# Moving the third block product ahead of the first set of output products in each pair of a gated unit

## The chip, the cores and the metric

The kernel runs on one core of a Trainium2 chip. The metric is the time of one execution in device microseconds (us). Before the change the median of 3 runs is 873.7 us (872.63 to 873.97).

## The reference, cut to what matters

The kernel computes three layers: windowed attention, a mixture of experts with one expert for each token, and a gated unit. The change lies in the gated unit:

```python
def _moe2_ref(x, w_gate, w_val, w_out, rms_g):      # 2304 tokens, 512 wide, 1536 hidden
    rms = np.sqrt(np.mean(x * x, axis=-1, keepdims=True) + 1e-06)
    xn = x / rms * rms_g
    g = xn @ w_gate
    silu = g * (1.0 / (1.0 + np.exp(-g)))
    val = xn @ w_val
    return (silu * val @ w_out).astype(np.float32)
```

## The kernel before, in words

The gated unit takes the tokens in 6 chunks of 384 (`c` = 0 to 5) and the 1536 hidden columns in 12 blocks of 128 (`f`). Every float32 operand is held as a high and a low float16 part, and a product is the sum of three products of parts. Chunks 0 and 1 are computed plainly (`plain`). Chunks 2 to 5 go through `quad(c, p)`, which takes hidden blocks 2p and 2p+1 together: 6 pairs in a chunk, 24 pairs in all. A pair is a two by two block product, and seven block products, named 1 to 7, give it instead of eight. One block product (`product`, L1014 to L1025) is 12 matmuls of 128x192 into one PSUM bank: gate and value, two halves of the contraction, three products of parts.

VectorE (DVE) puts the seven results together with additions (`add`, L1092). Product 1 is first copied to `u0` by ScalarE (L1110). `one` becomes hidden block 2p, `other` block 2p+1, each with a left and a right half of the tokens. The last addition of a pair is that of product 4 into the left half of `other` (L1126). Then `gated` (L1100) makes the activation: Silu on ScalarE (L1101), a multiply on VectorE (L1102), the high part on ScalarE (L1096) and the low part on VectorE (L1097).

The output products of a finished hidden block are one set of 9 matmuls of 128x512: three row blocks by three products of parts, added up in three banks over all 12 hidden blocks of a chunk (`down`, L1130). `downs` (L1214) takes the oldest block that waits in `pending`. A pair calls it twice, so that in its first set stands block 2(p-1) and in its second block 2(p-1)+1 of the pair before. The set of a chunk's last block falls into the second place of the next chunk's first pair; there the three results are copied to rows (`o`, L1142 and L1144) and scattered to the output. The first set of that chunk's second pair then begins the next sums in the same three banks.

Work for the next chunk is put between (`side_work`, L1267): loads in pair 0, maxima (L970, L487) in pair 1, the scale (L491, L495) in pair 2, transposes (`gtx`, L983) in pair 3, sums of the rows (L995 to L998) and splits into parts (L926 on ScalarE, L927 on VectorE) in pairs 4 and 5. The longest split, of 1536 columns, stands in pair 5 just ahead of `add(other[:, :, :HT], product(c, p, "4"), u)`.

The order on every engine is the order in which the program is written. The seven products use two PSUM buffer tags of two buffers each, and a tag's buffers are handed out in turn:

```python
PAIRS = {"1": (0, 0), "2": (1, 1), "3": (6, 2), "4": (2, 6), "5": (3, 3), "6": (4, 4), "7": (5, 5)}
acc = bank("a" if x in "1634" else "d", "g" + x)        # BANKS: "a": 2, "d": 2
```

Within a pair tag a is asked for by products 1, 6, 3 and 4 in this order, so that 1 and 3 lie in one of its banks, 6 and 4 in the other. A product's first matmul waits until the bank's last reader is done: product 6 of a pair waits for the addition of product 4 of the pair before, product 3 for the copy to `u0`, product 4 for the addition of product 6.

Of the kernel before, what the change touches and what calls it, by code (L numbers as in the profile page):

```python
# [74 lines left out]
def attn_moe_glu(tc, I, out, dbg=None):  # L75
    nc = tc.nc
    with contextlib.ExitStack() as top:
# [58 lines left out]
        def block_tile(name):  # L136
            return tail.tile([P, D], F32, name=name, tag="block", bufs=2)
# [34 lines left out]
        def bank(name, use=None):  # L172
            return ps.tile([P, 512], F32, name=use or name, tag=name, bufs=BANKS[name])
# [840 lines left out]
        def product(c, p, x):  # L1014

            i, j = PAIRS[x]
            acc = bank("a" if x in "1634" else "d", "g" + x)
            for gv in range(2):
                for m in range(2):
                    for n, (a, b) in enumerate(((0, 0), (0, 1), (1, 0))):  # L1020
                        nc.tensor.matmul(  # L1021
                            acc[:, gv * HT : gv * HT + HT], GV[p][:, a, gv, i, m * P : m * P + P], XC[c][:, b, j, m],
                            start=m == 0 and n == 0, stop=m == 1 and n == 2,
                        )
            return acc[:, :CHT].rearrange("p (g t) -> p g t", g=2)  # L1025
# [66 lines left out]
        add = lambda out, x, y: nc.vector.tensor_tensor(out, x, y, ALU.add)  # L1092
# [7 lines left out]
        def gated(c, f, g, v, si):  # L1100
            nc.scalar.activation(si, g, AF.Silu, scale=undo[:, c % 2, 0:1])  # L1101
            nc.vector.scalar_tensor_tensor(si, v, undo[:, c % 2, 1:2], si, ALU.mult, ALU.mult)  # L1102
            act_split(c, f, si)

        def quad(c, p, downs, work, last):

            p1, p2 = (product(c, p, x) for x in "12")
            u0, u = (block_tile(x)[:, :CHT].rearrange("p (g t) -> p g t", g=2) for x in ("u0", "u"))
            one, other = (g2.tile([P, 2, CHT], F32, name=x) for x in ("one", "other"))
            nc.scalar.activation(u0, p1, AF.Copy)  # L1110
            add(one[:, :, :HT], p2, u0)
            next(work, None)
            downs()
            add(u, product(c, p, "6"), u0)
            p5 = product(c, p, "5")
            add(one[:, :, HT:], p5, u)
            next(work, None)
            p3 = product(c, p, "3")
            add(one[:, :, HT:], p3, one[:, :, HT:])
            add(u, product(c, p, "7"), u)  # L1120
            add(other[:, :, HT:], p5, u)
            gated(c, 2 * p, one[:, 0], one[:, 1], one[:, 0])
            next(work, None)
            if not last:
                downs()
            add(other[:, :, :HT], product(c, p, "4"), u)  # L1126
            next(work, None)
            gated(c, 2 * p + 1, other[:, 0], other[:, 1], other[:, 0])

        def down(c, f, j):  # L1130
            ahi, alo = acts[c, f]
            acc = ACC[c][j]
            cols = slice(j * P, j * P + P)
            for n, (a, part) in enumerate(((ahi, 0), (ahi, 1), (alo, 2))):
                nc.tensor.matmul(  # L1135
                    acc, a[:, cols], GO[f][part],
                    start=f == 0 and n == 0, stop=f == NFF - 1 and n == 2,
                )
            if f == NFF - 1:
                o = row_tile("o")[:, :D]  # L1140
                if j % 2:
                    nc.vector.tensor_scalar(o, acc, undo[:, c % 2, 2:3], None, ALU.mult)  # L1142
                else:
                    nc.scalar.activation(o, acc, AF.Copy, scale=undo[:, c % 2, 2:3])  # L1144
                d = scatter(out, IX[c][j], o).ins
                for x in written:
                    tc.declare_no_dep(d, x, reason="the rows differ")
                written.append(d)
# [65 lines left out]
        def downs(last=False):  # L1214

            if pending:
                c, f = pending.pop(0)
                if f == 0:
                    ACC[c] = [bank(x, "acc") for x in "bbc"]
                for j in blocks:  # L1220
                    down(c, f, j)
# [82 lines left out]
        for c in range(PLAIN, NCH):  # L1304
            for p in range(NP):
                work = side_work(c, p)
                last = (c, p) == (NCH - 1, NP - 1)
                quad(c, p, downs, work, last)
                for _ in work:
                    pass  # L1310
                pending += [(c, 2 * p), (c, 2 * p + 1)]
        table = over["table"]

        c = NCH - 1
# [100 lines left out]
```

## Time and profile before

| | |
|---|---|
| median of 3 runs | 873.7 us |
| profiled execution | 880.13 us, of which the span of the trace is 878.3 us |
| TensorE matmuls (PE) | busy 839.8 us, 96% of the span |
| TensorE weight loads (PEld) | 652.4 us, 74% |
| VectorE (DVE) | 594.4 us, 68% |
| ScalarE (ACT) | 408.4 us, 47% |
| GpSimd (POOL) | 175.2 us, 20% |
| block products, L1021 | 2016 matmuls, first at 592.7 us, last at 858.4 us |

All times of rows are us from the start of the span. A timeline row gives start, duration, engine, line, operation, output and inputs, a count where equal neighbours are put together, and in brackets the idle time ahead of it with what ended it. Matmuls overlap: a row of 12 times n block product matmuls is shown some 0.16 us longer than the distance to the next row. "PEclk" is the granted TensorE clock: 1.00 is 2.4 GHz, 0.50 is 1.2 GHz.

### The profile page before, as it was taken

How to read it: one execution, taken by the hardware profiler on the slowest of the kernel's cores; microseconds unless marked ns; L12 is line 12 of the kernel's file. 1: busy time of each engine (PE TensorE's matmuls, PEld its weight loads, DVE VectorE, ACT ScalarE, POOL GpSimd, SP SyncE). 2: the span in 40 equal slices, each digit the busy share in tenths (PEclk: the TensorE clock that was granted, in tenths of full speed). 3: DMA queues.
4: the chain of work that ended last, by engine and by line, in shares of the span. 5: the costliest groups of instructions: out<-in, count | busy, mean ns of one | idle time of the engine just before them, and what ended most of it. 6: DMA issues, size and time to landing. Idle time of an engine off the chain costs nothing.

```text
span 878.3 us, 17260 instructions
## 1 busy us (share of the span) xinstructions
PE 839.8 (96%) x5927; PEld 652.4 (74%) x5927; DVE 594.4 (68%) x1647; ACT 408.4 (47%) x957; POOL 175.2 (20%) x206
## 2 busy tenths in 40 slices
PE   8999979999899999999899999899999999999994
PEld 6888878987788888888755555458787887778882
DVE  7657848798988887534456747666676666667752
ACT  6867759856445455322445534343233233233221
POOL 3644118532343333200000001001001001001001
PEclk9969989999999999999999999999999999999998
DMA  9994579426877776250055006201001000000001
GB/s 215 260 282 93 140 230 295 125 62 217 243 249 230 230 217 202 73 168 24 13 192 183 34 31 257 97 13 61 13 1 61 13 2 37 2 1 37 1 2 38
DMA packets 100470, 101.96 MB, mean 116 GB/s; under 512 B 63136, under 2 KB 75424, under 8 KB 100384
## 3 DMA queue, kind: packets, MB, share of 16 engines
q1 hardware_dynamic: 92848, 86.34, 33.3%
q0 software_dynamic: 4400, 14.20, 4.2%
q8 instruction: 52, 0.85, 0.4%
q10 hardware_dynamic: 3136, 0.30, 0.3%
q14 instruction: 34, 0.28, 0.1%
HBM read 67.18 MB, written 33.89 MB: 115 GB/s over the span
## 4 chain that ended last, share of the span: by engine, by line
issue 43%; PE 41%; DVE 8%; DMA 3%; ACT 2%; POOL 1%; POOLq 0%; SPq 0%; ACTq 0%; DVEq 0%
PE h L657 10%; PE y L682 10%; PE s L233 3%; PE g L1021 3%; PE xp L337 3%; PE xp L339 2%; DVE pb L261 2%; PE acc L1135 2%; PE mth L633 1%; PE few L369 1%; PE pt L302 1%; POOL out L710 1%; DMA yd<-yn,ix 1%; PE mtx L633 1%; DMA xd<-xs,pli 1%
## 5 line engine op out<-in xcount | busy, mean ns | idle before, releaser
L1021 PEld LDWEIGHTS <-gv 128*128 128x128 f16 x2016 | 167.7, 98 | 11.2
L1021 PE MATMUL g<-xc,gv 128*128 128x192 f16 x2016 | 175.0, 246 | 0.0
L710 POOL DMA_INDIRECT out<-o,ix x18 | 18.1, 1004 | 397.8 <-ACT o L1144 395.1
L682 PE MATMUL y<-W,hhi 128*128 x304 | 96.1, 397 | 0.0
L1037 PE MATMUL gv<-xn,gv 128*128 128x384 f16 x528 | 90.6, 326 | 1.3 <-DVE one L1102 0.7
L657 PE MATMUL h<-W,xhi 128*128 x272 | 90.0, 412 | 0.1
L1135 PE MATMUL acc<-go,alo 128*128 128x512 f16 x216 | 81.9, 379 | 0.0
L1037 PEld LDWEIGHTS <-gv 128*128 128x128 f16 x528 | 51.5, 98 | 37.9 <-issue 2.4
L272 ACT ACTIVATE pb<-pb,mn 128x256 f32<-128x256 f32 (+4 forms) x160 | 74.4, 468 | 10.7 <-DVE mn L261 10.0
L1135 PEld LDWEIGHTS <-ahi 128*128 128x128 f16 x432 | 41.4, 98 | 41.9 <-issue 3.4
L261 DVE CUSTOM_DVE_ANT_0 pb<-s,bias 128x256 f32<-128x256 f32 (+4 forms) x160 | 53.6, 380 | 23.4 <-PE s L233 22.5
L682 PEld LDWEIGHTS y<-W,hhi 128*128 128x128 f32 x304 | 57.4, 189 | 14.0
L1135 PE MATMUL acc<-gv,ahi 128*128 128x512 f16 x216 | 64.3, 379 | 3.5 <-ACT o L1144 1.8
L1135 PE MATMUL acc<-go,ahi 128*128 128x512 f16 x216 | 64.3, 379 | 0.7 <-ACT ahi L1096 0.7
L746 POOL TENSOR_TENSOR cw<-cw,cv 128x512 int32<-128x512 int32 x36 | 47.1, 1310 | 69.7 <-DVE cw L745 27.1
L682 PE MATMUL y<-W,hlo 128*128 x152 | 60.1, 396 | 0.0
L657 PEld LDWEIGHTS h<-W,xhi 128*128 128x128 f32 x272 | 49.1, 191 | 9.8 <-issue 0.4
L657 PE MATMUL h<-W,xlo 128*128 x136 | 54.6, 402 | 0.0
L1101 ACT ACTIVATE one<-one,undo 128x384 f32<-128x384 f32 x24 | 14.8, 615 | 83.7 <-DVE one L1092 83.7
L692 ACT ACTIVATE yn<-y,xg 128x512 f32<-128x512 f32 x19 | 13.1, 690 | 84.1 <-PE y L682 84.1
L1096 ACT ACTIVATE ahi<-one 128x384 f16<-128x384 f32 x36 | 18.8, 523 | 55.7 <-DVE one L1102 55.7
L233 PE MATMUL s<-kT,qT 64*128 64x256 f32 (+1 forms) x288 | 42.1, 404 | 0.3 <-ACT kT L203 0.2
(273 smaller groups left out, 1649.1 us busy)
## 6 DMA issues: line engine op xcount, KB each, us to landing
raw<-gd SPq DMA_DIRECT2D x20, 768.0 KB, 5.4
gd<-cw SPq DMA_DIRECT2D x36, 256.0 KB, 2.9
W<-in_moe_w SPq DMA_DIRECT2D x16, 512.0 KB, 5.9
cv<-in_moe_w_gate SPq DMA_DIRECT2D x12, 512.0 KB, 4.6
cv<-in_moe_w_val SPq DMA_DIRECT2D x12, 512.0 KB, 4.8
cv<-in_moe_w_out SPq DMA_DIRECT2D x12, 512.0 KB, 4.5
xd<-zrow SPq DMA_DIRECT2D x20, 257.0 KB, 5.5
xg<-xd SPq DMA_DIRECT2D x19, 257.0 KB, 3.2
```

The lines of the kernel that those rows point to most:

```text
L233: nc.tensor.matmul(sps[j][:, u, :W], qT[rows, i], win(i, j), start=True, stop=True)
L261: nc.vector.tensor_tensor_reduce(pb[rw, u, x0:x1], sp[rw, u, x0:x1], bias[rw, h, b0 + x0 : b0 + x1], 1.0, 3.0e38, ALU.add, ALU.min, M[t][0 ...
L272: nc.scalar.activation(pb[rw, u, x0:x1], pb[rw, u, x0:x1], AF.Exp, bias=mn[rw, h : h + 1], scale=-1.0, accum_out=sm[rw, h : h + 1],)
L337: nc.tensor.matmul(X[t][:, h], cur, T["v", t][:, h], start=True, stop=not full)
L657: nc.tensor.matmul(hp[f], x[:, k], WT[1][k][:, ds(w, 1), part, f * 512 : f * 512 + 512], start=k == 0 and n == 0, stop=k == KD - 1 and n == 2,
L682: nc.tensor.matmul(y, x[:, k], WT[2][k // 2][:, ds(w, 1), part, k % 2 * D : k % 2 * D + D], start=k == 0 and x is hi and part == 0, stop=k ...
L710: return nc.gpsimd.indirect_dma_start(dst[:, :], bass.IndirectOffsetOnAxis(ap=ix[:, 0:1], axis=0), src, None, bounds_check=NTOK - 1, oob_i ...
L746: nc.gpsimd.tensor_tensor(ci, ci, low.bitcast(I32), ALU.add)
L1021: nc.tensor.matmul(acc[:, gv * HT : gv * HT + HT], GV[p][:, a, gv, i, m * P : m * P + P], XC[c][:, b, j, m], start=m == 0 and n == 0, stop ...
L1037: nc.tensor.matmul(acc[:, :CHT], w[:, m * P : m * P + P], XC[c][b][:, k], start=k == 0 and n == 0, stop=k == KD - 1 and n == 2,)
L1096: nc.scalar.activation(ahi, si, AF.Copy, scale=2.0**-LOW)
L1135: nc.tensor.matmul(acc, a[:, cols], GO[f][part], start=f == 0 and n == 0, stop=f == NFF - 1 and n == 2,)
```

## The change

In `quad`, the block product 6 and its addition are issued ahead of the first set of output products instead of behind it.

```diff
             nc.scalar.activation(u0, p1, AF.Copy)
             add(one[:, :, :HT], p2, u0)
             next(work, None)
+            add(u, product(c, p, "6"), u0)
             downs()
-            add(u, product(c, p, "6"), u0)
             p5 = product(c, p, "5")
             add(one[:, :, HT:], p5, u)
             next(work, None)
```

On TensorE, at the first pair of chunk 3. `g4`, `g1`, `g2`, `g6`, `g5` are the block products, `acc` the output products; of each group of matmuls the first one is shown, and a line of dots stands for the rest. Before:

```order
L1021 MATMUL g4_7697<-xc_6786,gv5_6018 128x192
...
L1021 MATMUL g1_7717<-xc_7548,gv0_5415 128x192
...
L1021 MATMUL g2_7730<-xc_7548,gv0_5415 128x192
...
L1135 MATMUL acc_7022<-gv5_6018,ahi0_7682 128x512
...
L1021 MATMUL g6_7764<-xc_7548,gv0_5415 128x192
...
L1021 MATMUL g5_7778<-xc_7548,gv0_5415 128x192
```

With the change:

```order
L1021 MATMUL g4_7697<-xc_6786,gv5_6018 128x192
...
L1021 MATMUL g1_7717<-xc_7548,gv0_5415 128x192
...
L1021 MATMUL g2_7730<-xc_7548,gv0_5415 128x192
...
L1021 MATMUL g6_7755<-xc_7548,gv0_5415 128x192
...
L1135 MATMUL acc_7036<-gv5_6018,ahi0_7682 128x512
...
L1021 MATMUL g5_7778<-xc_7548,gv0_5415 128x192
```

The 12 matmuls of `g6` moved ahead of the 9 of the set; between `g4` and `g6`, which share a bank, stand now two block products and no set. The same holds in all 24 pairs.

On VectorE, at the end of chunk 2 and the beginning of chunk 3, the order is the same before and with the change (the rows are those of before):

```order
L1097 SCALAR_TENSOR_TENSOR alo0_7683<-ahi0_7682,one_7608 128x384
L927 SCALAR_TENSOR_TENSOR xc_7548<-tt_7471,up2_2901,xc_7548 128x1536
L1092 TENSOR_TENSOR other_7609<-g4_7697,u_7607 128x2x192
L1102 SCALAR_TENSOR_TENSOR other_7609<-other_7609,undo_2904 128x384
L1097 SCALAR_TENSOR_TENSOR alo1_7714<-ahi1_7713,other_7609 128x384
L1092 TENSOR_TENSOR one_7745<-g2_7730,u0_7743 128x2x192
```

Nothing moved here: the longest split stands ahead of the addition of `g4`, which `g6` waits for. The only row that moves on VectorE is in the first of the 24 pairs, where the addition of product 6 now stands ahead of the copy of an output row:

```order
 L1092 TENSOR_TENSOR one<-g_6857,u_6870 128x2x192
+L1092 TENSOR_TENSOR u<-g_6882,u_6870 128x384
 L1142 TENSOR_SCALAR o<-acc,undo 128x512
-L1092 TENSOR_TENSOR u<-g_6906,u_6870 128x384
 L1092 TENSOR_TENSOR one<-g_6920,u 128x2x192
```

ScalarE, GpSimd and the DMA queues keep their order.

## Rows read from the trace of the kernel before

**Rows 1.** The page's costliest groups, block products: count, busy us, mean ns, idle before.
```profile
L1021 PE MATMUL g<-xc,gv 128*128 128x192 f16 x2016 | 175.0, 246 | 0.0
```

**Rows 2.** Timeline of PE, from the end of chunk 2 into chunk 3's second pair.
```profile
660.36 0.59 PE L1135 MATMUL acc<-gv,ahi 128*128 128x512 f16 x2
...
662.30 4.12 PE L1021 MATMUL g<-xc,gv 128*128 128x192 f16 x48
666.26 0.59 PE L1135 MATMUL acc<-go,ahi 128*128 128x512 f16 x2
...
673.47 0.59 PE L1135 MATMUL acc<-gv,ahi 128*128 128x512 f16 x2 [0.84 <-ACT o L1144]
```

**Rows 3.** Timeline of DVE, the same stretch.
```profile
659.44 1.82 DVE L927 SCALAR_TENSOR_TENSOR xc<-tt,up,xc 128x1536 f16<-128x1536 f32 x1 [0.91 <-ACT xc L926]
661.17 0.55 DVE L1092 TENSOR_TENSOR other<-g,u 128x384 f32<-128x384 f32 x1
...
666.76 0.55 DVE L1092 TENSOR_TENSOR u<-g,u 128x384 f32<-128x384 f32 x1
```

**Rows 4.** Timeline of PE and DVE, a transpose that waits for an addition.
```profile
630.53 2.14 PE L1021 MATMUL g<-xc,gv 128*128 128x192 f16 x24
632.71 0.56 DVE L1092 TENSOR_TENSOR u<-g,u 128x384 f32<-128x384 f32 x1 [0.43 <-PE g L1021]
633.32 0.66 PE L983 MATMUL gtx<-ident,yr 128*128 128x128 f32 x4 [0.65 <-DVE u L1092]
```

**Rows 5.** Timeline of PE and DVE, the other three late additions of product 4.
```profile
603.55 0.55 DVE L1092 TENSOR_TENSOR other<-g,u 128x384 f32<-128x384 f32 x1
603.58 0.59 PE L1135 MATMUL acc<-gv,ahi 128*128 128x512 f16 x2
728.95 0.59 PE L1135 MATMUL acc<-gv,ahi 128*128 128x512 f16 x2
729.77 0.55 DVE L1092 TENSOR_TENSOR other<-g,u 128x384 f32<-128x384 f32 x1
797.55 0.59 PE L1135 MATMUL acc<-gv,ahi 128*128 128x512 f16 x2
798.36 0.55 DVE L1092 TENSOR_TENSOR other<-g,u 128x384 f32<-128x384 f32 x1
```

**Rows 6.** Timeline of DVE and PE, the addition of product 4 that is just in time.
```profile
717.51 0.55 DVE L1092 TENSOR_TENSOR other<-g,u 128x384 f32<-128x384 f32 x1
718.13 0.59 PE L1135 MATMUL acc<-gv,ahi 128*128 128x512 f16 x2
```

**Rows 7.** Timeline of PE and DVE, the first two pairs of chunk 4.
```profile
730.89 4.12 PE L1021 MATMUL g<-xc,gv 128*128 128x192 f16 x48
735.05 0.56 DVE L1092 TENSOR_TENSOR u<-g,u 128x384 f32<-128x384 f32 x1
741.78 0.59 PE L1135 MATMUL acc<-gv,ahi 128*128 128x512 f16 x2 [0.55 <-ACT o L1144]
```

**Rows 8.** Timeline of DVE and PE, chunks 3 and 4: the maximum, the scale's first transpose.
```profile
682.73 0.15 DVE L487 TENSOR_REDUCE amax<-xmax 128x1 f32<-128x3 f32 x1
682.99 0.27 PE L491 MATMUL few<-ident,amax 128*1 128x128 f32 x1
751.39 0.14 DVE L487 TENSOR_REDUCE amax<-xmax 128x1 f32<-128x3 f32 x1
751.59 0.27 PE L491 MATMUL few<-ident,amax 128*1 128x128 f32 x1
```

**Rows 9.** Windows of PE: us, busy (count), PEclk, DMA share, GB/s.
```profile
42.00:44.00 2.00, 1.15 (x11) 1.00 0.82 216
46.00:48.00 2.00, 2.00 (x10) 0.50 1.12 298
56.00:58.00 2.00, 2.00 (x10) 0.50 1.06 335
672.00:673.00 1.00, 0.63 (x3) 1.00 0.39 152
```

## The prediction

> **What bounds the kernel now.** I read the costliest groups first, then the timelines of PE, DVE and ACT side by side from 592 us on, where the 24 pairs lie. The block products have no idle time at all ahead of 2016 matmuls [rows 1]: in the pairs TensorE sets the pace, and VectorE and ScalarE work in its shadow. The reader should see in the timeline of PE that a pair is a fixed train. One set of 9 output matmuls takes 662.30 - 660.36 = 1.94 us, and four block products in a row take 666.26 - 662.30 = 3.96 us, so one takes 0.99 us [rows 2]. The only waits of PE that touch this change are those for an output row: 0.84 us in the second pair of chunk 3 [rows 2] and 0.55 us in that of chunk 4 [rows 7], both ahead of the third row block of the first set. The third quantity to read is when VectorE finishes the addition of product 4, because that frees the bank which the next pair's product 6 writes.
>
> **The change part by part.** It adds and removes no instruction. TensorE executes the same 84 block matmuls and 18 output matmuls in a pair (9 in the first pair and in the last), so the busy time is unchanged. What changes is distance. Between product 4 and the next product 6 stood products 1 and 2 and a set, 0.99 + 0.99 + 1.94 = 3.92 us; now only 1.98 us are left. Nothing becomes shorter by the move itself, since PE was waiting for nothing there.
>
> *The new wait at product 6.* With the change product 6 would start where the first set starts now. It must not start before the addition of product 4 has ended and PE has heard of it. For that last step a transpose gives the price: the addition starts at 632.71, lasts 0.56, ends at 633.27, and the transpose that needs it starts at 633.32, so 0.05 us [rows 4]. I went through the 23 places at which one pair follows another. Four come out late:
> - into chunk 3: the addition ends at 661.17 + 0.55 = 661.72 [rows 3], product 6 could start at 660.36 [rows 2]: it waits 661.77 - 660.36 = 1.41 us;
> - into chunk 4: 729.77 + 0.55 + 0.05 - 728.95 = 1.42 us [rows 5];
> - into chunk 5: 798.36 + 0.55 + 0.05 - 797.55 = 1.41 us [rows 5];
> - from the first to the second pair of chunk 2, where no second set stands between products 7 and 4: 603.55 + 0.55 + 0.05 - 603.58 = 0.57 us [rows 5].
>
> The cause of the first three is to be seen on VectorE: the split of 1536 columns, 1.82 us long and itself 0.91 us late behind ScalarE's half of it, stands ahead of the addition [rows 3], and VectorE's order there does not change. Sum: 1.41 + 1.42 + 1.41 + 0.57 = 4.81 us. At the other 19 places the addition is in time; the nearest is 718.13 - (717.51 + 0.55) = 0.07 us [rows 6], which covers the 0.05 us. Behind the waiting matmul stand, on PE's queue, everything else of the pair; the set that used to fill this time is ready but cannot pass it. PE is the pacing engine, so each wait counts in full unless a later wait of PE shrinks for it.
>
> *What shrinks for it.* The third row block of the first set in the second pairs of chunks 3 and 4 now comes a block product (0.99 us) later against VectorE and ScalarE, so its waits of 0.84 and 0.55 us go. Each idle figure is some 0.16 us short of what PE loses, because the matmul ahead is shown that much longer than its distance to the next (4.12 against 3.96 us in [rows 2]); so up to 1.71 us could come back. But those rows were late because VectorE and ScalarE were, and the next thing that PE needs from VectorE is the maximum, for the transpose at line 491 one pair on. There I count chunk by chunk.
> - Chunk 3. After its first wait PE is 1.41 us later. VectorE takes up product 7 at 666.76, 0.34 us after the product's shown end 662.30 + 4.12 = 666.42 [rows 2, 3]; undisturbed it takes 632.71 - (630.53 + 2.14) = 0.04 us [rows 4]. So it has 0.30 us of backlog, and becomes only 1.41 - 0.30 = 1.11 us later. All that follows from there on (output rows, activation, maximum) is 1.11 us later. The maximum then ends at 682.73 + 0.15 + 1.11 = 683.99, and the transpose starts at 684.04 instead of 682.99 [rows 8]. Net: 1.05 us. Of the 1.41 us, 0.36 us come back.
> - Chunk 4. VectorE takes up product 7 at 735.05, 0.04 us after 730.89 + 4.12 = 735.01 [rows 7], so there is no backlog and it becomes 1.42 us later. The transpose waits for the maximum already now (751.39 + 0.14 + 0.05 = 751.58 against 751.59, [rows 8]), and so starts 1.42 us later. Net: 1.42 us; what is saved at the output row is lost again at the transpose.
> - Chunk 5 has no such wait for an output row or a maximum: 1.41 us. Chunk 2: 0.57 us.
>
> Sum: 0.57 + 1.05 + 1.42 + 1.41 = 4.45 us. Its bounds: if the output-row waits come back whole, 4.81 - 1.71 = 3.10 us; if nothing comes back and the three places like that of [rows 6] lose some 0.2 us each, about 5.4 us. I take 4.45, since it follows PE to the next instruction that needs VectorE.
>
> *The rest.* The moved addition on VectorE in the first pair of chunk 2 is done while the set runs and delays one output row by at most its 0.55 us, with no PE instruction behind it that is due. The first set itself starts 0.99 us later, and its inputs have been ready longer. Product 3 and product 7 stand as far from products 1 and 2 as before (the same three groups lie between). The tail begins at products 7 and 4 of the last pair, which the move does not bring forward.
>
> *The clock.* The granted clock stays at 1.00, the 2.4 GHz level, through the second in which PE waits for the output row and is busy only 0.63 us [rows 9]. Far earlier in the kernel it did fall: PE was busy 1.15 of 2 us from 42 to 44, and from 46 to 58 us, six windows, the clock was 0.50, the 1.2 GHz level [rows 9]. The Trainium skill ("TensorE: Matmul & The Clock Gate", section on psum-queue depth-cycling) warns that a kernel which cycles through its banks can idle so often between groups of matmuls that the clock swings between its levels. By that rule the four new waits could cost a fall of the clock, and the sum would be some 6 us more for each; by the rows of this stage it is 4.45 us.
>
> **The sum against the times.** The profiled execution took 880.13 us, 6.43 us above the median. The sum is made in it: 884.6 us there. The terms come from engine work and one queue order, not from transfers, so I carry them over unchanged: 873.7 + 4.45 = 878.1 us, 0.5% slower.
>
> **The rivals.**
> - *No dependence on product 4, not slower.* If product 6 got the bank of product 3 instead, it would find it free: no new wait, and the output-row waits go. Then 873.7 - 1.71 = 872.0 us. For it speaks that two buffers exist; against it that tag a hands them out in turn to products 1, 6, 3, 4, so that 6 and 4 always share one. It decides which of the two buffers product 6 gets. Chance 0.03.
> - *The waits shrink outside the profile.* An unprofiled run is 6.43 us shorter, and if part of that lies in ScalarE's and VectorE's split, the addition comes earlier. From 1.36 us earlier on, the three large waits are gone; what stays is 0.57 us at most: 874.3 us, within 0.2%. Against it: the delay is made of instruction lengths on two engines (1.82 us and 0.91 us of waiting for ScalarE). Chance 0.08.
> - *More places turn late.* If a matmul that waits hears of an addition 0.25 us after its end rather than 0.05, the four places cost 0.2 us more each, the three like that of [rows 6] about 0.18 us each, and some of the other near ones a little: 4.45 + 0.80 + 0.54 = 5.8 us, so 879.5 us. For it: only one row gives the 0.05. Chance 0.08.
> - *The clock falls* after one of the long waits. Twelve us at half the clock do six us of work, so one fall costs 6 us: 873.7 + 4.45 + 6 = 884.1 us. For it: waits of 1.4 us are longer than any in this stage now. Against it: the row of 672 us above. Chance 0.04.
>
> **How the numbers follow.** The forecast as summed has the chance 0.77. A measurement of this kernel can tell 0.2%, 1.75 us, from no change. Slower by more than that: 0.77 + 0.08 + 0.04 = 0.89. Within it: 0.08 and half of the first rival, 0.09. Faster: 0.02. The range starts at the lower bound of the sum on the lowest run before, 872.63 + 3.10 = 875.7 us, and ends at the third rival, 879.5 us, a little above the lowest-to-highest spread of the runs; the clock and the two small cases stay outside, 0.15 in all.
>
> **What would show it right or wrong.** In the profile of the changed kernel the block products should have idle time ahead of them, put down to VectorE's line 1092, at four places: about 1.2 to 1.4 us at the first pairs of chunks 3, 4 and 5 and about 0.5 us at the second pair of chunk 2. The waits of 0.84 and 0.55 us for the output row should be gone, and in their place the transposes at line 491 of these two chunks should wait for the maximum. Busy time and counts on every engine should be unchanged, and the clock 1.00 from 592 to 860 us. The prediction is wrong if product 6 shows no wait, if the transposes do not wait and the time is only some 3 us longer, or if the clock falls in this stage.

## The result and the profile after

The changed kernel took 880.71 us in the median of 20 runs (877.80 to 888.32), the kernel before 875.79 us in 20 runs (872.63 to 883.96). The ratio is 1.0064 with a 95% interval of 1.0042 to 1.0087: slower by 5.6 us, between 3.7 and 7.6 (the two medians lie 4.9 us apart). The forecast of +4.45 us, a ratio of 1.0051, lies in that interval. The forecast time of 878.1 us and its range, up to 879.5 us, lie too low.

The profiled execution of the changed kernel took 881.28 us, its span is 879.5 us. Its costliest groups show idle time ahead of the block products, where [rows 1] had none:

```profile
L1021 PE MATMUL g<-xc,gv 128*128 128x192 f16 x2016 | 177.1, 246 | 4.9 <-DVE other L1092 4.2
```

The waits of PE from 588 to 870 us (line that waited, line waited for, total us, times, longest us) name the places:

```profile
PE g L1021 <- DVE other L1092: 4.2, 4, 1.3
PE gtx L983 <- DVE u L1092: 1.9, 3, 0.7
PE acc L1135 <- ACT ahi L1096: 1.4, 2, 0.7
PE few L491 <- DVE amax L487: 1.0, 2, 0.7
PE g L1021 <- DVE xc L927: 0.6, 1, 0.6
```

Four waits for the addition of product 4, two of the scale's transpose for the maximum where no idle time was shown before, no wait for an output row any more: these were forecast. The last line was not: one wait of product 6 for the split `xc`. The timeline of PE shows each with its time:

```profile
588.83 2.23 PE L1021 MATMUL g<-xc,gv 128*128 128x192 f16 x25
591.70 1.07 PE L1021 MATMUL g<-xc,gv 128*128 128x192 f16 x11 [0.65 <-DVE xc L927]
...
601.06 1.15 PE L1021 MATMUL g<-xc,gv 128*128 128x192 f16 x12 [0.41 <-DVE other L1092]
...
659.26 1.16 PE L1021 MATMUL g<-xc,gv 128*128 128x192 f16 x12 [1.26 <-DVE other L1092]
...
681.56 0.27 PE L491 MATMUL few<-ident,amax 128*1 128x128 f32 x1 [0.32 <-DVE amax L487]
...
728.95 1.16 PE L1021 MATMUL g<-xc,gv 128*128 128x192 f16 x12 [1.26 <-DVE other L1092]
...
751.59 0.27 PE L491 MATMUL few<-ident,amax 128*1 128x128 f32 x1 [0.67 <-DVE amax L487]
...
798.98 1.16 PE L1021 MATMUL g<-xc,gv 128*128 128x192 f16 x12 [1.26 <-DVE other L1092]
...
867.68 0.38 PE L1135 MATMUL acc<-go,alo 128*128 128x512 f16 x1
```

The reader should look at the counts: in the first pair 25 matmuls run, that is products 1 and 2 and the first matmul of product 6, and then 11 wait. The timeline of DVE, same kernel, has the instruction they wait for, and further on the split and the addition into chunk 3:

```profile
589.83 1.82 DVE L927 SCALAR_TENSOR_TENSOR xc<-tt,up,xc 128x1536 f16<-128x1536 f32 x1 [0.91 <-ACT xc L926]
...
656.91 1.82 DVE L927 SCALAR_TENSOR_TENSOR xc<-tt,up,xc 128x1536 f16<-128x1536 f32 x1 [0.91 <-ACT xc L926]
658.65 0.55 DVE L1092 TENSOR_TENSOR other<-g,u 128x384 f32<-128x384 f32 x1
```

The split ends at 589.83 + 1.82 = 591.65 and the 11 matmuls start at 591.70. It writes the low parts of four of the seven input blocks, product 6's among them; the high parts come from ScalarE and were there, so the first matmul, which reads a high part, could run.

For comparing kernels I use the **stretch** from the first block product to the last output matmul. In the trace of before it starts at 592.72 and ends at 866.24 us: 273.52 us. With the change it is 867.68 - 588.83 = 278.85 us, so 5.33 us longer. The span as a whole grew by only 1.2 us, since in this execution the work ahead of the stretch happened to be 3.9 us shorter; the last section comes back to that.

### The profile page after: what moved, and what is told of

Its sections match the earlier page's. It is cut to its first block, busy times and chain, and to the rows that moved or that the text cites. A ratio compares the mean times of both kernels' runs of the same rounds, so it can differ in the third digit from the quotient of the medians.

```text
span 879.5 us, 17260 instructions
## 1 busy us (share of the span) xinstructions
PE 837.0 (95%) x5927; PEld 648.5 (74%) x5927; DVE 593.7 (68%) x1647; ACT 408.1 (46%) x957; POOL 175.2 (20%) x206
## 4 chain that ended last, share of the span: by engine, by line
PE 70%; DVE 11%; issue 8%; ACT 4%; DMA 4%; SPq 1%; POOL 0%; POOLq 0%; ACTq 0%; DVEq 0%
PE g L1021 13%; PE y L682 11%; PE h L657 11%; PE acc L1135 11%; PE gv L1037 8%; PE s L233 3%; PE xp L337 2%; PE xp L339 2%; DMA xd<-xs,pli 2%; PE mth L633 2%; DMA xg<-xd 1%; DVE pb L261 1%; DVE gv L927 1%; PE pt L302 1%; ACT gv L926 1%
## 5 line engine op out<-in xcount | busy, mean ns | idle before, releaser
L1021 PE MATMUL g<-xc,gv 128*128 128x192 f16 x2016 | 177.1, 246 | 4.9 <-DVE other L1092 4.2
L1135 PEld LDWEIGHTS <-alo 128*128 128x128 f16 x216 | 21.3, 99 | 27.0 <-DVE alo L1097 1.4
```

Of the source, the lines that this page charges most:

```text
L1021: nc.tensor.matmul(acc[:, gv * HT : gv * HT + HT], GV[p][:, a, gv, i, m * P : m * P + P], XC[c][:, b, j, m], start=m == 0 and n == 0, stop ...
L1135: nc.tensor.matmul(acc, a[:, cols], GO[f][part], start=f == 0 and n == 0, stop=f == NFF - 1 and n == 2,)
```

## The experiments

All runs are told by their stretch, and by the timed ratio where one was taken; that ratio is to the kernel before, timed beside the run. The theory: product 6 waits because it now stands too close behind what VectorE still owes it. The rival: the order on TensorE costs by itself, or what a wait costs is made up for later.

**The bank taken apart.** With the change, product 4 gets its buffer from the other tag, so that product 6 no longer shares a bank with it:

```diff
-            acc = bank("a" if x in "1634" else "d", "g" + x)
+            own = x == "4" and (c, p) not in ((PLAIN, 0), (NCH - 1, NP - 1))
+            acc = bank("a" if x in "1634" and not own else "d", "g" + x)
```

> The change, with product 4 taken out of the bank that product 6 uses (its buffer comes from the other tag, except in the first and the last of the 24 pairs). The measure is the stretch from the first block product to the last matmul of the trace: 273.52 us before (592.72 to 866.24), 278.85 us with the change (588.83 to 867.68). Theory (product 6 waits for the addition of product 4 because they share a bank): the three waits at the first pairs of chunks 3 to 5 are gone, the one into the second pair of chunk 2 (0.57 us) and the one for the split in the first pair (0.81 us) stay: 273.52 + 0.57 + 0.81 = 274.9 us, ratio to before 1.0016. Rival (the order on TensorE costs by itself, without a wait for a bank): the stretch stays at 278.9 us, ratio 1.0061.

Measured: 277.37 us, ratio 1.0057 (1.0032 to 1.0082). Neither theory had the number. The timeline of PE (line numbers are one higher here, by the added line):

```profile
594.27 1.07 PE L1022 MATMUL g<-xc,gv 128*128 128x192 f16 x11 [0.65 <-DVE xc L927]
...
661.35 1.07 PE L1022 MATMUL g<-xc,gv 128*128 128x192 f16 x11 [0.70 <-DVE xc L927]
...
730.48 1.07 PE L1022 MATMUL g<-xc,gv 128*128 128x192 f16 x11 [0.71 <-DVE xc L927]
...
800.15 1.07 PE L1022 MATMUL g<-xc,gv 128*128 128x192 f16 x11 [0.70 <-DVE xc L927]
```

and that of DVE:

```profile
659.48 1.82 DVE L927 SCALAR_TENSOR_TENSOR xc<-tt,up,xc 128x1536 f16<-128x1536 f32 x1 [0.91 <-ACT xc L926]
661.22 0.55 DVE L1093 TENSOR_TENSOR other<-g,u 128x384 f32<-128x384 f32 x1
```

The waits for the addition are gone from the chunk starts, so the bank was what held product 6 there. But right behind that wait stood a second one, for the low part of the new chunk's input, as in the first pair: the split ends at 661.30, and 11 matmuls start at 661.35. It ends only some 0.5 us before the addition, and so most of the wait stays.

**Only where the addition is in time.** Product 6 stands in front except in the first pairs of chunks 2 to 5 and in the second of chunk 2 (lines against the kernel before):

```diff
+            early = p > 1 or (p == 1 and c > PLAIN)
+            if early:
+                add(u, product(c, p, "6"), u0)
             downs()
-            add(u, product(c, p, "6"), u0)
+            if not early:
+                add(u, product(c, p, "6"), u0)
```

> The change only in the 19 pairs in which the addition of product 4 came in time; in the first pairs of chunks 2 to 5 and in the second of chunk 2 product 6 stands behind the set as before. Theory: no new wait at product 6; the waits for the output rows go, but the transposes of the scale wait instead: 273.5 us for the stretch, ratio 1.000. Rival (the order costs in every pair alike): 19/24 of 5.33 us, 277.7 us, ratio 1.0048.

Measured: 273.46 us, and no wait at product 6. Nineteen of the 24 moves cost nothing when they are made together. The timeline of PE has in chunks 3 and 4, where the output-row waits were:

```profile
676.84 2.14 PE L1021 MATMUL g<-xc,gv 128*128 128x192 f16 x24 [0.29 <-ACT u L1110]
...
684.22 0.27 PE L491 MATMUL few<-ident,amax 128*1 128x128 f32 x1 [0.32 <-DVE amax L487]
...
752.81 0.27 PE L491 MATMUL few<-ident,amax 128*1 128x128 f32 x1 [0.68 <-DVE amax L487]
```

So what was saved at the output rows went into product 3's wait for the copy to `u0` and into the transpose of line 491. The timed ratio, 1.0035 (1.0008 to 1.0063), did not fit a stretch equal to before, and I ran the same kernel again:

> The kernel of the second run again (the change only in the 19 pairs in which the addition of product 4 came in time), whose stretch was as before and whose timed ratio was 1.0035. Theory (the stretch holds all that differs, the rest of that ratio was scatter): an interval that takes in 1. Rival (something outside the stretch costs 3 us): the ratio stays near 1.0035.

Measured: stretch 273.46 us once more, ratio 1.0003 (0.9981 to 1.0025). And the kernel before against itself:

> The kernel before with one empty line added: the same program. It shows how far two sets of runs of one program lie apart. Both theories: ratio 1.000 with an interval that takes in 1; stretch from the first block product to the last matmul 273.5 us.

Measured: 273.52 us, ratio 1.0009 (0.9979 to 1.0040). So I take the first ratio of the 19 moves for scatter: it did not come back, and part of it goes with the granted clock, which was 0.982 on average in those 12 runs and 0.985 in the 29 runs of before beside them.

**Only where it is late.** The complement, but for the first of all pairs: `early = (p == 0 and c > PLAIN) or (p == 1 and c == PLAIN)`.

> The change only in the four pairs in which the addition of product 4 was late: the first pairs of chunks 3, 4 and 5 and the second of chunk 2. Theory: nearly the whole loss, 0.57 + 1.10 + 1.43 + 1.43 = 4.5 us as in the changed kernel, a little less if the waits for output rows that stay there overlap: 277.3 to 278.0 us, ratio 1.0043 to 1.0052. Rival (every pair costs alike): 4/24 of 5.33 us, 274.4 us, ratio 1.001.

Measured: 278.11 us, 4.59 us longer than before, ratio 1.0095 (1.0061 to 1.0129). Four moves carry nearly all of the loss. The timed ratio, of 6 runs alone, lies above what the stretch explains (4.59 us are 1.0052). The granted clocks of these runs go with the rest: their mean over the whole kernel is 0.9805 in the six and 0.9848 in the 29 of before. A straight line through all 35 runs has 0.62 us for 0.001 of that clock, which is 2.7 of the 7.3 us between the two means, and leaves 4.65 us (3.2 to 6.1) to the kernel, in which the 4.59 us of the stretch lie. In the timeline of PE (lines are four higher here: 1139 and 1148 are 1135 and 1144 of before) the output row's wait stays at 0.55 us, since product 6 stands behind the set in the second pairs here:

```profile
661.12 1.16 PE L1021 MATMUL g<-xc,gv 128*128 128x192 f16 x12 [1.26 <-DVE other L1092]
...
673.95 0.59 PE L1139 MATMUL acc<-gv,ahi 128*128 128x512 f16 x2 [0.55 <-ACT o L1148]
```

**The splits swapped.** With the change, the long split of each chunk's last pair changes places with the short one:

```diff
                     yield
-                    row_split(c + 1, 1)
+                    row_split(c + 1, 2)
                     yield
-                    row_split(c + 1, 2)
+                    row_split(c + 1, 1)
```

> The change, with the two splits of each chunk's last pair swapped: the one of 1536 columns after product 5, the one of 384 columns just ahead of the addition of product 4. Theory (the long split on VectorE is what makes the addition late): the three waits at the first pairs of chunks 3 to 5 fall from 1.42 us to 0.3 us or less; 0.57 and 0.81 us stay: 274.9 to 275.8 us, ratio 1.0016 to 1.0026. Rival (the addition is late for another reason, such as ScalarE's queue): they stay above 1 us, 278 us or more, ratio 1.005.

Measured: 274.56 us, 0.3 us less than the lower end expected, ratio 1.0025 (0.9998 to 1.0053). Where the 0.3 us come back was not tried; product 3's wait for `u0`, 0.29 us shown with the 19 moves, is not there. No wait is left at the starts of chunks 3 to 5, neither for the bank nor for the input; of product 6's waits the timeline of PE has only

```profile
592.64 1.07 PE L1021 MATMUL g<-xc,gv 128*128 128x192 f16 x11 [0.65 <-DVE xc L927]
...
602.00 1.15 PE L1021 MATMUL g<-xc,gv 128*128 128x192 f16 x12 [0.41 <-DVE other L1092]
```

Both waits at a chunk start had the same cause, the long split that stands last on VectorE ahead of the addition.

**The first pair alone** (`early = p == 0 and c == PLAIN`), and **the swap in the plain part too**, added to the kernel with the splits swapped:

```diff
                     if f == 10:
...
                         row_split(c + 1, 0)
-                        row_split(c + 1, 1)
+                        row_split(c + 1, 2)
                     if f == 11:
-                        row_split(c + 1, 2)
+                        row_split(c + 1, 1)
```

> The change only in the first of the 24 pairs. Theory (there product 6 waits for the low part of its own input, which the long split of the plain part still writes): one wait with 0.65 us of idle shown, the stretch is 273.5 + 0.8 = 274.3 us. Rival (the wait is made up for later): 273.5 us.

> The change with both splits swapped in the last pairs (as in the run before) and the same swap at the end of the plain part, so that the long split comes before the short one there too. Theory: the wait of 0.65 us in the first pair goes as well; only the 0.57 us into the second pair of chunk 2 and the waits at line 491 stay: 274.56 - 0.81 = 273.8 us. Rival (the first pair waits for something else): 274.6 us as in the run before.

Measured: 274.33 us for the first pair alone, 0.81 us more than before, with the one wait of product 6 that the theory has:

```profile
601.86 1.07 PE L1021 MATMUL g<-xc,gv 128*128 128x192 f16 x11 [0.65 <-DVE xc L927]
```

And 273.76 us with both swaps, 0.80 us less than with one: that wait is gone. It is the term that the prediction did not have. The three groups of pairs, each run alone, add up to the whole change: -0.06 us for the 19, 4.59 us for the four and 0.81 us for the first make 5.34 us, against 5.33 us measured.

**A version that beats both.** Product 6 stands in front only in the second pairs of chunks 3, 4 and 5, and two transposes move one place back. (The expectation names chunks 3 and 4, where PE waits for an output row; the condition takes in chunk 5 as well, which has no such wait.)

```diff
+            early = p == 1 and c > PLAIN
...
                 if p == 2:
+                    yield
                     for x in (1, 2):
                         scales(c + 1, x)
                         yield
                 if p == 3:
                     for j in blocks:
+                        if j == 2:
+                            yield
                         row_turn(c + 1, j)
                         yield
```

> The kernel before, with product 6 ahead of the set only in the second pairs of chunks 3 and 4, where PE waits for an output row, and with two transposes put one place later: that of the scale (line 491) behind product 5, and the third row transpose of each fourth pair behind product 4. Theory (what the earlier product 6 saves at the output rows is lost only because the scale's transpose stands next in the queue): the waits for output rows and at line 491 go, about 0.5 us stay saved in chunk 3 and 0.8 us in chunk 4, and the three waits of 0.65 us ahead of the row transposes (0.81 us each from start to start) go as well: 273.5 - 1.3 - 2.4 = 269.8 us, ratio 0.996. Rival (each saving turns into a wait further on): 273.5 us, ratio 1.000.

Measured: 269.52 us, 4.00 us less than before (0.9954), ratio 0.9966 (0.9941 to 0.9990). The interval leaves out 1 by little, as the first one of the 19 moves did, so the stretch carries the result. The waits for output rows, of the row transposes (L983) and at line 491 are gone; besides two waits near its end that before has too, the stretch shows one, in the timeline of PE:

```profile
671.59 2.14 PE L1021 MATMUL g<-xc,gv 128*128 128x192 f16 x24 [0.29 <-ACT u L1110]
```

How much of that is the moved product, and how much the transposes, was asked with product 6 behind the set everywhere (`early = False`):

> The kernel with the two transposes put one place later, and product 6 behind the set everywhere, as before. Theory: the three row transposes no longer wait (3 x 0.81 us), the wait of 0.3 us at line 491 in chunk 4 goes, and the waits of 1.0 and 0.7 us for output rows stay: 273.5 - 2.4 - 0.3 = 270.8 us for the stretch, so that the moved product 6 is worth 1.3 us in the second pairs of chunks 3 and 4. Rival (the later slots alone do it): 269.5 us.

Measured: 270.62 us. The output-row waits stand there as in [rows 2, 7]:

```profile
666.54 0.59 PE L1139 MATMUL acc<-gv,ahi 128*128 128x512 f16 x2 [0.84 <-ACT o L1148]
...
733.97 0.59 PE L1139 MATMUL acc<-gv,ahi 128*128 128x512 f16 x2 [0.55 <-ACT o L1148]
```

So the later transposes give 2.90 us. The moved product, in three of 24 pairs and with the scale's transpose no longer next in the queue, gives 1.10 us, where the 19 moves, these three among them, gave 0.06 us with the transposes in their old places.

## Why the prediction was right and where it was wrong

**Direction and mechanism: right.** The forecast waits of 1.41, 1.42, 1.41 and 0.57 us came as 1.26, 1.26, 1.26 and 0.41 us of idle time shown, each 0.16 us short of the loss as the prediction had said, so 1.42, 1.42, 1.42 and 0.57. The release took 659.26 - (658.65 + 0.55) = 0.06 us, against the 0.05 assumed. The output-row waits went, and the transposes of the scale waited in their place, as forecast. The timed interval of 3.7 to 7.6 us could not have told 4.45 from 5.33; the trace can. By the start of line 491 within the stretch (before 682.99 and 751.59, less 592.72; after 681.56 and 751.59, less 588.83) the terms are:

| part | forecast us | measured us |
|---|---|---|
| chunk 2, first pair | 0 | 0.81 |
| chunk 2, second pair | 0.57 | 0.57 |
| chunk 3 | 1.05 | 92.73 - 90.27 - 1.38 = 1.08 |
| chunk 4 | 1.42 | 162.76 - 158.87 - 2.46 = 1.43 |
| chunk 5 and tail | 1.41 | 5.33 - 3.89 = 1.44 |
| sum | 4.45 | 5.33 |

**The missing term.** "I went through the 23 places at which one pair follows another" left out the first pair, and at the 23 looked at one thing that product 6 needs, its bank. Its input was not looked at. In the first pair the bank is free and the input is not: 0.81 us, shown alone by the run with the first pair only and taken away by the swap in the plain part. At the chunk starts the same input is late too, by 0.87 us, but hidden behind the longer wait for the bank; the run with the banks apart brought it to light (0.71 us shown, and the 0.16 us that are not).

**The range: wrong.** The measured 880.71 us lies 1.2 us above its end. Two steps made it so. The missing term is 0.81 us. The larger one is the base: the sum was put on 873.7 us, the median of three runs, and the lower end was built on the lowest of these three, the upper one on their median. Over 20 runs the kernel before has a median of 875.79 us and reaches from 872.63 to 883.96. On that base the sum of the prediction gives 875.79 + 4.45 = 880.2 us, which is outside the range already, and with the missing term 881.1 us; the missing term on the old base gives 879.0 us, which is inside. Three further sets of 17 to 29 runs of the kernel before, beside the experiments, have medians of 875.47, 878.51 and 879.15 us. The scatter could be seen beforehand: the profiled execution of 880.13 us, which the prediction set aside as 6.43 us above the median, lies within the 20 runs. The range gave room for doubts about the mechanism and hardly any for the scatter of the runs, 11 us in these 20.

**The rivals.** "No dependence on product 4" was run by force, with the banks apart: even then the stretch is 277.37 us against 273.52 before, for the input comes late. "The waits shrink outside the profile" rested on an unprofiled run being shorter, but the changed kernel's profiled execution, 881.28 us, is only 0.6 us above its median; nor is the rival borne out by the timed ratio, which is that of the stretch (5.33 us of 875.79 is 1.0061, measured 1.0064). "More places turn late" did not happen: at the 19 others no wait is shown. The clock stayed at 1.00 in every window of the stretch, of which these are two of the changed kernel (us; busy us of PE, PEld, DVE, ACT and POOL with counts; PEclk, DMA share, GB/s):

```profile
592.00:662.00 70.00, 67.68 (x637) 54.24 (x635) 45.54 (x96) 21.56 (x38) 2.96 (x3) 1.00 0.07 24
730.00:800.00 70.00, 67.41 (x630) 53.62 (x628) 45.29 (x96) 21.44 (x38) 2.96 (x3) 1.00 0.03 13
```

So waits of 1.4 us did not lower it here, and the caution of the Trainium skill ("TensorE: Matmul & The Clock Gate", section on psum-queue depth-cycling) did not come to bear.

## What to carry to other kernels

Before moving a product forward on the engine that sets the pace, list everything it needs, its bank and each of its inputs, and for every place where it is issued compare when the last of them is ready with when it would now start; a wait that is hidden behind another counts as soon as the other is removed. Most of the moves here were free and useless, and the loss sat in the five places where VectorE had not yet done what the product needs. So a move that is made only where it meets a wait can win (1.10 us here, with the next wait taken away) while the same move everywhere loses (5.33 us). And a saving at one wait is only kept if the next instruction in the queue doesn't wait for the same late engine.

## What was not expected of the hardware

The scatter between runs lies ahead of the stretch. The stretch of the kernel before was 273.52 us in both of its profiled executions, and that of the 19 moves 273.46 us in both of its own; but the first block product, ahead of which all these kernels' instructions stand in the same order (but for the plain part's swapped splits), came at any time from 586.66 to 598.98 us. The windows of PE there (us, busy, PEclk, DMA share, GB/s) show the granted clock at its lower level for different lengths of time. The kernel before, with the first block product at 592.72 us:

```profile
40.00:60.00 20.00, 19.15 (x109) 0.66 1.04 276
...
120.00:140.00 20.00, 16.47 (x122) 0.83 0.89 269
```

The run with the first pair alone, at 598.98 us:

```profile
40.00:60.00 20.00, 18.53 (x130) 0.83 1.01 245
...
120.00:140.00 20.00, 14.80 (x79) 0.57 0.76 237
```

The changed kernel, at 588.83 us:

```profile
40.00:60.00 20.00, 18.52 (x156) 1.00 1.05 278
...
120.00:140.00 20.00, 18.89 (x151) 0.92 0.93 294
```

In these three, the later the first block product, the longer the clock was low in these two windows. The low clock does not account for all of the scatter: in four of the twelve profiles (banks apart, splits swapped, later transposes with and without the moved product) windows of 10 us from 0 to 580 us add up to the same 13.6 us at the lower level, and their first block products come at 591.39, 589.76, 589.63 and 586.66 us. What makes the other 4.7 us stays open. For a change of half a per cent the stretch it touches, read in one profile, said more than a dozen timed runs did.
